# Two VectorE transposes per K tile instead of eight, and TensorE's closing code placed before its loop, in a decode kernel that streams a KV cache

## The chip, the cores and the metric

The kernel runs on one core of a Trainium2 chip. The metric is device microseconds of one execution. A profile is taken of one execution (of before a further one, at 1277.19 us; of each other kernel one of its timed runs). Its span is about 1.3 to 1.6 us shorter than the time of that same execution, and its timestamps are what the traces below show. Before took 1277.59 us (median of 3 runs, 1277.06 to 1277.76) when the prediction was made. All outputs were correct.

## The reference, cut to what matters

One token goes through a mix of two blocks: attention over a cache of 65,536 positions, and a small gated feed-forward block. K and V together are 537 MB of bf16; everything else is 12 MB.

```
x: (1, 1, 448)   k_cache, v_cache: (1, 8, 65536, 256)   wq: (448, 4096)   wo: (4096, 448)
q = x @ wq                                  # 16 heads of 256, two per K/V head
p = softmax(q . k / 16);  o = p . v
a = o.reshape(1, 1, 4096) @ wo
b = ((relu(x @ W_gate)) * (x @ W_up)) @ W_down
g = sigmoid(sum(x * gate_w))
return g * a + (1 - g) * b
```

## The kernel before: the parts that the change touches

K and V come in as 8 MB tiles, 32 of each, into a ring of three buffers. A K tile lands as 128 partitions x 32,768 bf16. VectorE transposes it in place, as uint32, in eight instructions. Scores of the first half of the tile wait for the first four, those of the second half for the last four.

```python
def f_trans(sl, w):
    v = ring[sl][:, w * 4096:(w + 1) * 4096].bitcast(U32)      # 128 x 2048 uint32
    return lambda e: e.transpose(v, v)
# ... (cut) ... for every K tile n in ring slot sl:
kd = dma("sp", t, "r%d" % sl, lambda e, n=n, sl=sl: e.dma_start(ring[sl][:], k_src(n)), free(("k", n)))
tr = [op("dv", tk + 2.22 * w, f_trans(sl, w), [kd]) for w in range(8)]
for b in range(2):
    qk[n, b] = op("pe", tk + (9 * (b + 1) if n else 20 + b), f_qk(n, b, sl), [tr[4 * b + 3], xcopy, ...])
```

The second argument of `op` is a planned time; it only orders the instructions of one engine. VectorE, ScalarE, SyncE and GpSimd run straight code. TensorE has a loop over the heads, between opening code and closing code (last V tiles, output projection):

```python
pl.emit("pe", pe[:heads[0][0]], nc.tensor)       # opening code
pl.emit_loop(H + 1, span, nc.tensor, go)         # the loop; GpSimd gives it one "go" per step
pl.emit("pe", pe[end:], nc.tensor)               # closing code
```

The compiled program has 1940 instructions for TensorE, 465 for VectorE, 186 for GpSimd, 150 for ScalarE, 106 for SyncE.

## Time and profile before

| | before |
|---|---|
| time, span of the profile | 1277.59 us, 1275.7 us |
| moved, mean rate | 549 MB, 430 GB/s over the span |
| DMA share and rate, 200 to 1200 us | 1.00, 433 GB/s |
| VectorE busy, of it transposes | 637 us, 565 us |
| VectorE waiting for K tiles | 390 us |

In all views PE is TensorE's matmuls, PEld its weight loads, DVE VectorE, ACT ScalarE, POOL GpSimd; SPq and PEq are the instruction sequencers of SyncE and TensorE. From the page of before: the slices of DMA (40 equal parts of the span, tenths busy), the queues (packets, MB, share of 16 engines' time) and the costliest group (line, engine, operation, shapes, count, busy us, mean ns, idle before and what ended it).

```profile
DMA  9999999999999999999999999999999999999998
...
q1 hardware_dynamic: 12034, 549.03, 99.6%
q8 instruction: 7, 0.11, 0.0%
q14 instruction: 6, 0.05, 0.0%
...
L369 DVE STREAM_TRANSPOSE ring<-ring 128x2048 uint32<-128x2048 uint32 x256 | 565.4, 2275 | 390.0 <-DMA ring<-in_A_k_cache_dram 390.0
```

The DMA engines are the limit (share 1.00 at 433 GB/s from 200 to 1200 us), and VectorE waits for them (390.0 us). Two queues carry instructions, not data, with a share that rounds to nothing. By what follows, q8 is TensorE's. The 8 KB fetches are q14's.

The stretches of before: bounds in us and length, busy us of PE, PEld, DVE, ACT, POOL, then granted clock, DMA share of 16 engines, GB/s.

```profile
200.00:1200.00 1000.00, 319.73 (x3542) 119.70 (x3534) 503.83 (x313) 48.49 (x94) 0.00 (x0) 0.61 1.00 433
1200.00:1270.00 70.00, 28.77 (x345) 12.25 (x345) 9.07 (x14) 3.14 (x8) 0.00 (x0) 0.68 0.99 421
1270.00:1271.00 1.00, 0.56 (x4) 0.09 (x4) 0.12 (x1) 0.00 (x0) 0.00 (x0) 0.68 0.75 289
1271.00:1272.00 1.00, 0.63 (x8) 0.35 (x8) 0.57 (x1) 0.00 (x0) 0.00 (x0) 0.50 0.33 127
1272.00:1273.00 1.00, 1.00 (x16) 0.53 (x12) 0.16 (x1) 0.00 (x0) 0.00 (x0) 0.50 0.07 25
```

Read the DMA share of the last line: 0.07 is about one engine of sixteen. After 1272 us one DMA engine alone still moves data, and TensorE's last weights wait for it (shown below). With a share of 1.00, in the long stretch, the sixteen move 433 GB/s.

One period of before in the timeline (start us, length us, engine, line, operation, shapes, count, idle time before and its releaser), lines of other engines left out:

```profile
510.67 0.33 SPq L577 DMA_DIRECT2D ring<-in_A_v_cache_dram  x1
...
515.17 0.33 SPq L510 DMA_DIRECT2D ring<-in_A_k_cache_dram  x1
527.88 17.66 DVE L369 STREAM_TRANSPOSE ring<-ring 128x2048 uint32<-128x2048 uint32 x8 [16.51 <-DMA ring<-in_A_k_cache_dram]
```

When the V load is issued at 510.67 us, the K tile queued ahead of it needs until 527.88 us. So in this period 17 us of transfers are queued when a buffer is given back. From that I estimate that a buffer may come up to 17 us later, or sooner, without the queue running dry.

The end of before in the chain of waits (start us, length, what):

```profile
1249.20 22.12 DMA ring<-in_A_wo_dram
1271.33 0.04 issue
1271.37 0.91 PE A_ps L391 x8
1272.28 0.20 PE M_ps L426 x4
1272.48 1.65 PE A_ps L391 x15
1274.12 0.02 issue
1274.15 0.38 DVE P_sb L619
```

The chain merges the last matmuls into one piece (x15) and so hides the last wait. The timeline shows it, at TensorE's last weight loads:

```profile
1273.57 0.09 PEld L391 LDWEIGHTS A_ps<-ring,attnT 128*1 128x1 bf16 x4 [0.30 <-DMA ring<-in_A_wo_dram]
```

They wait for the last piece of `wo`. Its last packet ends at 1273.08 us (next section), and they start 0.5 us later.

### What the DMA records say beyond the views

The trace also holds a record of every DMA packet (start, length, size, queue) but not which of the sixteen engines moved it. It can be worked out. Every engine moves the same 752 packets of the data queue, 80 transfers closed by a 4-byte packet each, and an engine starts a packet within some nanoseconds (mostly 3 to 4 in before) of the end of its last one. Following size and adjacency gives sixteen chains. Their numbering is arbitrary, and two engines that pass within some 10 ns can be exchanged. For each engine I read how far it lies behind the first one when both close the same transfer. Here are the lags of before at the closing of four transfers, each row sorted, and the instruction fetches during data transfer:

```
at   33.8 us: 0 to 0.73
at  138.1 us: 0 .11 .12 .12 .14 .29 .36 .73 .80 1.28 1.67 1.99 2.01 2.02 2.03 2.03
at  447.7 us: 0 .12 .13 .20 .35 .77 .84 .88 1.00 1.66 1.98 2.00 2.01 2.02 2.02 2.28
at 1237.1 us: 0 .12 .26 .35 .41 .92 .98 1.02 1.14 1.71 2.01 2.03 2.05 2.06 2.06 3.39

16 KB (q8, TensorE): 53.9  63.6  70.8  78.1  85.3  106.8  1263.8 us, seven different DMA engines
 8 KB (q14), on the engine that ends last: 58.6  415.1  868.4 us
 8 KB (q14), on three other engines: 426.3  438.2  1254.4 us
last packet of data ends 1273.08 us; the second-to-last engine ends at 1271.77 us
```

A 16 KB fetch leaves its engine about 1.55 us further behind, an 8 KB one 0.97 us (those on the engine that ends last) or 0.7 us (the others). The lag then stays (five engines at 1.99 to 2.03 us at 138.1 us; five at 2.01 to 2.06 at 1237.1), with a DMA share of 1.00 from 200 to 1200 us: no engine idles in which to catch up. The engine with three 8 KB fetches ends 1.3 us after all others.

### The profile page before, as it was taken

How to read it: one execution, taken by the hardware profiler on the slowest of the kernel's cores; microseconds unless marked ns; L12 is line 12 of the kernel's file. 1: busy time of each engine (PE TensorE's matmuls, PEld its weight loads, DVE VectorE, ACT ScalarE, POOL GpSimd, SP SyncE). 2: the span in 40 equal slices, each digit the busy share in tenths (PEclk: the TensorE clock that was granted, in tenths of full speed). 3: DMA queues.
4: the chain of work that ended last, by engine and by line, in shares of the span. 5: the costliest groups of instructions: out<-in, count | busy, mean ns of one | idle time of the engine just before them, and what ended most of it. 6: DMA issues, size and time to landing. Idle time of an engine off the chain costs nothing. (4 is left out here: it accounts for less than half of the span.)

```text
span 1275.7 us, 10235 instructions
## 1 busy us (share of the span) xinstructions
PE 423.0 (33%) x4572; PEld 162.0 (13%) x4572; DVE 636.7 (50%) x432; ACT 63.3 (5%) x124; POOL 4.3 (0%) x21
## 2 busy tenths in 40 slices
PE   3333422334123432225331243322433314233235
PEld 1201110111001210012110111100111101011012
DVE  2697633465533555434555444555435655336600
ACT  0001000010000100001000010000100001000000
POOL 1000000000000000000000000000000000000000
PEclk8656566656566565666665666656666556666667
DMA  9999999999999999999999999999999999999998
GB/s 402 447 427 428 440 429 440 432 429 429 438 440 432 430 429 438 436 432 436 427 429 440 438 432 432 429 438 434 432 438 427 440 429 436 436 429 429 424 437 352
DMA packets 12051, 549.20 MB, mean 430 GB/s; under 512 B 1283, under 2 KB 1798, under 8 KB 3078
## 3 DMA queue, kind: packets, MB, share of 16 engines
q1 hardware_dynamic: 12034, 549.03, 99.6%
q8 instruction: 7, 0.11, 0.0%
q14 instruction: 6, 0.05, 0.0%
q10 hardware_dynamic: 4, 0.00, 0.0%
HBM read 549.03 MB, written 0.00 MB: 430 GB/s over the span
## 5 line engine op out<-in xcount | busy, mean ns | idle before, releaser
L369 DVE STREAM_TRANSPOSE ring<-ring 128x2048 uint32<-128x2048 uint32 x256 | 565.4, 2275 | 390.0 <-DMA ring<-in_A_k_cache_dram 390.0
L380 PE MATMUL ST<-ring,xc 128*16 128x512 bf16 x2048 | 225.2, 613 | 738.4 <-PEq L86 738.4
L380 PEld LDWEIGHTS ST<-ring,xc 128*16 128x16 bf16 x2048 | 68.6, 120 | 880.7 <-issue 879.0
L411 PE MATMUL O<-ring,ptp 128*4 128x512 bf16 x2048 | 150.5, 457 | 36.6 <-PEq L86 24.4
L521 ACT ACTIVATE P_sb<-ST,nmb 128x512 bf16<-128x512 f32 x32 | 45.2, 1412 | 1101.7 <-DVE nmb L519 1101.7
L519 DVE TENSOR_REDUCE nmb<-ST 128x1 f32<-128x512 f32 x32 | 22.0, 689 | 117.8 <-PE ST L380 117.8
L411 PEld LDWEIGHTS O<-ring,ptp 128*4 128x4 bf16 x2048 | 57.5, 100 | 129.1 <-issue 81.3
L421 DVE CAST o_sb<-O 128x512 bf16<-128x512 f32 x8 | 5.5, 691 | 78.2 <-PE O L411 78.2
L540 DVE TENSOR_TENSOR P_sb<-P_sb,hs 128x1024 bf16<-128x1024 bf16 x16 | 18.9, 1221 | 9.6 <-ACT hs L534 9.6
L545 PE MATMUL PT<-identb,P_sb 128*128 128x128 bf16 x128 | 16.2, 307 | 16.8 <-PEq L86 15.8
L545 PEld LDWEIGHTS PT<-identb,P_sb 128*128 128x128 bf16 x128 | 12.4, 138 | 19.2 <-issue 19.2
L554 ACT COPY ptp<-PT 128x256 bf16<-128x256 bf16 x32 | 10.3, 375 | 23.9 <-PE PT L545 23.9
L343 PE MATMUL QN<-ring,P_sb 128*128 128x512 bf16 x32 | 9.9, 486 | 3.9 <-DMA ring<-in_A_wq_dram 3.9
L521 ACT ACTIVATION_READ_ACCUMULATOR P_sb<-ST,nmb 128x1 f32 x32 | 8.4, 262 | 0.0
L458 DVE STREAM_TRANSPOSE scr<-P_sb 128x256 uint32<-128x256 uint32 x1 | 0.4, 445 | 14.3 <-ACT P_sb L457 14.3
L478 PE MATMUL QN<-ring,xT 128*1 128x448 bf16 x16 | 1.7, 568 | 16.1 <-DMA ring<-in_B_W_up_dram 16.1
L433 PE MATMUL M_ps<-emat,o_sb 128*64 128x1 bf16 x112 | 4.5, 199 | 6.6 <-PEq L86 6.6
L530 PE MATMUL M_ps<-identf,hs 128*2 128x128 f32 x8 | 2.6, 321 | 11.1 <-PEq L86 11.1
L440 DVE TENSOR_SCALAR attnT<-M_ps,hs 64x4 bf16<-64x4 f32 x14 | 3.1, 220 | 6.3 <-PE M_ps L433 6.2
L566 DVE RECIPROCAL hs<-M_ps 128x2 f32<-128x2 f32 x8 | 1.4, 170 | 8.3 <-PE M_ps L565 8.3
L433 PEld LDWEIGHTS M_ps<-emat,o_sb 128*64 128x64 bf16 x112 | 4.1, 154 | 9.9 <-issue 9.9
L532 PE MATMUL M_ps<-mx,nselT 2*128 2x1 f32 x16 | 3.6, 292 | 4.1 <-PEq L86 4.1
(80 smaller groups left out, 71.4 us busy)
## 6 DMA issues: line engine op xcount, KB each, us to landing
ring<-in_A_v_cache_dram SPq DMA_DIRECT2D x1, 4096.0 KB, 46.7
ring<-in_A_wq_dram SPq DMA_DIRECT2D x1, 3072.0 KB, 10.6
ring<-in_A_wo_dram SPq DMA_DIRECT2D x1, 2240.0 KB, 37.4
ring<-in_A_v_cache_dram SPq DMA_DIRECT2D x1, 2048.0 KB, 17.8
ring<-in_B_W_down_dram SPq DMA_DIRECT2D x1, 1568.0 KB, 20.8
ring<-in_B_W_gate_dram SPq DMA_DIRECT2D x1, 1344.0 KB, 32.3
ring<-in_B_W_up_dram SPq DMA_DIRECT2D x1, 1344.0 KB, 35.0
ring<-in_A_v_cache_dram SPq DMA_DIRECT2D x1, 1024.0 KB, 19.9
```

Of the source, the lines that this page charges most:

```text
L343: ins = e.matmul(QN_ps, xw3[:, k_, 31 - h:159 - h], rhs, start=(h == 0 and kt == 0), stop=(h == H - 1 and kt == R3))
L369: return lambda e: e.transpose(v, v)
L380: ins = e.matmul(bank[32 * w:32 * w + 16, :], xc[:, x0:x0 + 16], ktv[sl][:, u0:u0 + 16, c, :, r_], start=(b == 0 and c == 0 and r_ == 0), ...
L411: ins = e.matmul(OP[32 * g:32 * g + 4, :], ptp[:, col:col + 13:4], ring[sl][:, base + k * 512:base + (k + 1) * 512], start=(a == 0 and k < ...
L421: o1 = op("dv", tn, lambda e: e.tensor_copy(o_sb[:], OP[:]), [pv[n], last.get(("otr", h - 1))])
L433: ins = e.matmul(T_ps[64 * q:64 * q + 64, s:s + 1], o_sb[:, par * 256 + s:par * 256 + 256:4], emat[:, 2 * par + q:2 * par + q + 1], start= ...
L519: smax[n] = op("dv", tk + 22, lambda e, n=n, NM=NM, t_=t_: e.tensor_reduce(NM[:, t_:t_ + 1], ST[n % 2][:], AX.X, ALU.max, negate=True), [q ...
L521: aexp[n] = op("ac", tk + 23, lambda e, n=n, t_=t_, NM=NM, RS=RS: e.activation(P_sb[:, t_:2048:4], ST[n % 2][:], ACTF.Exp, bias=NM[:, t_:t ...
L532: h5 = mop("pe", T + 15, lambda e, h=h: e.matmul(NMR_ps, nselT[0:2, :], mx2[0:2, 0:1], start=True, stop=True), [h4, l_["ns"]])
L540: rsc = op("dv", tt, lambda e, X=X, pb=pb: e.tensor_tensor(pb, pb, X[:, 12:16].unsqueeze(1).to_broadcast([128, 256, 4]), ALU.mult), [h7, a ...
L545: ins = e.transpose(PT[rd][:, s * 128:(s + 1) * 128], P_sb[:, (rd * 8 + s) * 128:(rd * 8 + s + 1) * 128], identb[:, :])
L554: ins = e.copy(dst, src)
```

## The change

Its intent, as I read it: VectorE gets fewer, longer instructions; and TensorE's closing code is laid in memory before the loop instead of at the very end, so that its fetch leaves the tail. The outer loop runs twice: it skips the closing code and runs the head loop, then comes back and runs the closing code. The arithmetic is the same.

```diff
         def f_trans(sl, w):
-            v = ring[sl][:, w * 4096:(w + 1) * 4096].bitcast(U32)
+            v = ring[sl][:, w * 16384:(w + 1) * 16384].bitcast(U32)
             return lambda e: e.transpose(v, v)
 ...
-                tr = [op("dv", tk + 2.22 * w, f_trans(sl, w), [kd]) for w in range(8)]
+                tr = [op("dv", tk + 8.88 * w, f_trans(sl, w), [kd]) for w in range(2)]
 ...
-                    qk[n, b] = op(... f_qk(n, b, sl), [tr[4 * b + 3], xcopy, ...])
+                    qk[n, b] = op(... f_qk(n, b, sl), [tr[b], xcopy, ...])
 ...
-        pl.emit_loop(H + 1, span, nc.tensor, go)
-        pl.emit("pe", pe[end:], nc.tensor)
+        with nc.tensor.Fori(0, 2) as part:
+            with nc.tensor.If_eq(part.val.handles[0], 1):
+                pl.emit("pe", pe[end:], nc.tensor)
+            with nc.tensor.If_eq(part.val.handles[0], 0):
+                pl.emit_loop(H + 1, span, nc.tensor, go)
```

## The prediction

> **What bounds the kernel.** The DMA queue. The page's slices show DMA at 9 tenths throughout; by stretches it is 1.00 busy at 433 to 434 GB/s from 200 to 1200 us. [...] 549 MB at 434 GB/s is 1265 of the 1275.7 us. The chain of waits ends on the last A_wo pieces, then projections, casts and the store. In each 38.7 us period VectorE waits about 16.5 us for the K tile (waits, timeline). When a period's V load is issued (510.7 us), the K tile ahead of it still has 17 us to run (lands 527.9): the queue never runs dry.
>
> **VectorE.** Eight transposes of 128x2048 uint32 (2275 ns each, one every 2.21 us, 17.66 us per tile) become two of 128x8192. The other size in the trace is 256 elements, 445 ns: slope 1.02 ns an element. Estimate: 8.5 to 8.65 us each, 17.2 per tile; VectorE busy falls from 637 to about 620 us. The first half of the scores still waits for half a tile, 8.6 instead of 8.85 us. None of this is critical: slots come free half a microsecond sooner into a queue with 17 us of work. In tiles 0 to 3 the maximum may wait up to 4 us longer behind a transpose; no load is late for it.
>
> **Instruction fetch, the only way it can show.** The DMA records hold instruction fetches: seven of 16 KB for TensorE (six from 54 to 107 us, one at 1263.8, in the closing code) and 8 KB ones for the others (58.6, 415, 426, 438, 868, 1254 us). Following packets by size and adjacency on each DMA engine, I find that a 16 KB fetch sets its engine back about 1.5 us and an 8 KB one 0.65 to 1; the lag is never made up, since no engine idles. The engine that finishes last got three 8 KB fetches and ends at 1273.08; the next end at 1271.77. Six fewer transposes per tile remove 192 of VectorE's 465 instructions, one to two fetches. If one was on that engine, the end comes up to 1.3 us sooner; then engines that fetched for TensorE are last.
>
> Moving the closing code takes the fetch at 1263.8 out of the tail, but that engine is not the last and TensorE shows no idle time there: about 0. Two jumps are added. [...] The first comes around 61 us, before work ready at 72, the second at 1247, with 10 us of slack before the next V tile (1260.3). A fetch on an already late engine could cost 0.5 to 1.5 us.
>
> **Predicted:** 1276.8 us, 80% range 1274.8 to 1279.0. Faster by over 2%: 0.01; within 2%: 0.98; slower: 0.01.
>
> **What would show it.** Right: 64 transposes of about 8.6 us; VectorE's wait for K half a microsecond longer a tile; DMA still 434 GB/s; no instruction fetch near 1264 us, fewer 8 KB ones; last landing 0 to 1.3 us earlier. Wrong: transposes well over 9 us; DMA share below 1.00 between 200 and 1200; TensorE waiting for its sequencer after 1247; a last engine later than 1273.
>
> **What would make it wrong.** A fetch in the tail that stalls TensorE over 10 us, a transpose much dearer at this size, or fetches piling on one DMA engine.

Two sentences that no run of this case shows are cut from it, where marked; neither is a term of the sum. The sum came to 1276.8 us: 1277.59 us less 0.8, which lies between the 0 and the 1.3 us that the lags allow, with about 0 for the closing code.

## The result, and the profile after

| | before | after |
|---|---|---|
| time, median (range), 6 runs each | 1277.20 us (1277.06 to 1277.76) | 1276.32 us (1276.00 to 1276.48) |
| span of the profile | 1275.7 us | 1275.2 us |
| VectorE busy, of it transposes | 637 us, 565 us | 625 us, 554 us |
| VectorE waiting for K tiles | 390 us | 402 us |
| instructions of VectorE, of TensorE | 465, 1940 | 279, 1952 |

The ratio is 0.9992, 95% interval 0.9979 to 1.0005. A ratio is the mean time of one kernel's runs over that of the other's of the same rounds, so not quite the ratio of the medians. By the interval this is "the same"; the six runs of each do not overlap, and further below the medians of kernels that should be equal, by the theory tested there, agree to 0.2 us (the first result of after, up to 0.34 us higher, is the exception), which is why 0.9 us can be explained at all.

The page of after, the lines that answer to those of before:

```profile
DMA  9999999999999999999999999999999999999998
...
q8 instruction: 7, 0.11, 0.0%
q14 instruction: 5, 0.04, 0.0%
...
L369 DVE STREAM_TRANSPOSE ring<-ring 128x8192 uint32<-128x8192 uint32 x64 | 553.9, 8691 | 402.5 <-DMA ring<-in_A_k_cache_dram 402.5
```

VectorE gave back 11.5 us of transposes and waits 12.5 us longer for K tiles: the saved time became waiting. One 8 KB fetch less is the other difference on this page. The stretches of after:

```profile
200.00:1200.00 1000.00, 318.63 (x3546) 118.86 (x3538) 495.46 (x159) 48.48 (x94) 0.00 (x0) 0.61 1.00 433
...
1270.00:1271.00 1.00, 0.27 (x8) 0.13 (x6) 0.69 (x1) 0.00 (x0) 0.00 (x0) 0.77 0.71 272
1271.00:1272.00 1.00, 1.00 (x14) 0.50 (x12) 0.04 (x1) 0.00 (x0) 0.00 (x0) 0.50 0.33 124
1272.00:1273.00 1.00, 1.00 (x12) 0.48 (x8) 0.13 (x1) 0.00 (x0) 0.00 (x0) 0.50 0.04 14
```

The long stretch is the same to the GB/s. Again one engine is alone after 1272 us, and it stops sooner (share 0.04 instead of 0.07). By the DMA records it is not VectorE's engine any more. The timeline and the end of the chain of after:

```profile
528.31 17.30 DVE L369 STREAM_TRANSPOSE ring<-ring 128x8192 uint32<-128x8192 uint32 x2 [16.87 <-DMA ring<-in_A_k_cache_dram]
```

```profile
1247.32 23.46 DMA ring<-in_A_wo_dram
1270.78 0.04 issue
1270.82 0.91 PE A_ps L391 x8
1271.73 0.20 PE M_ps L426 x4
1271.93 1.67 PE A_ps L391 x15
1273.59 0.02 issue
1273.62 0.38 DVE P_sb L619
```

TensorE's last weight loads, in the timeline of after:

```profile
1273.04 0.09 PEld L391 LDWEIGHTS A_ps<-ring,attnT 128*1 128x1 bf16 x4 [0.29 <-DMA ring<-in_A_wo_dram]
```

The whole tail stands 0.5 us earlier and is otherwise the same chain. By the DMA records, VectorE's engine has two fetches (131.0 and 869.8 us) in place of three and lies 2.15 us behind at 1237 us (3.39 in before), no 16 KB fetch stands near 1264 us, and the last packet ends at 1272.58 us. The engine that ends last, 2.78 us behind, is another one: it was late from the start and then fetched for TensorE (see "The full change again"). This profile is of the slowest of the six runs of after (1276.48 us).

### The profile page after: what moved, and what is told of

Read it like the earlier page. It is cut to its first block, busy times and chain, and to the rows that moved or that the text cites. A ratio compares the mean times of both kernels' runs of the same rounds, so it can differ in the third digit from the quotient of the medians.

```text
span 1275.2 us, 10054 instructions
## 1 busy us (share of the span) xinstructions
PE 420.1 (33%) x4572; PEld 160.9 (13%) x4572; DVE 625.3 (49%) x240; ACT 63.3 (5%) x124; POOL 4.6 (0%) x21
## 5 line engine op out<-in xcount | busy, mean ns | idle before, releaser
L369 DVE STREAM_TRANSPOSE ring<-ring 128x8192 uint32<-128x8192 uint32 x64 | 553.9, 8691 | 402.5 <-DMA ring<-in_A_k_cache_dram 402.5
L391 PE MATMUL A_ps<-ring,attnT 128*1 128x224 bf16 x64 | 4.7, 305 | 1.3 <-DMA ring<-in_A_wo_dram 0.7
```

The costliest lines, as they stand in the source:

```text
L391: ins = e.matmul(A_ps[32 * g:32 * g + 1, 0:D2], lhsT, rhs[:, g * D2:(g + 1) * D2], start=start, stop=stop, skip_group_check=True, tile_pos ...
```

## The experiments

Theory A: the DMA is the limit, and the execution ends when the DMA engine that is furthest behind ends. VectorE's instruction fetches all go to one DMA engine; fewer instructions mean fewer fetches there. Rival B: the gain comes from the moved closing code. Rival C: it comes from the shorter time that VectorE needs per tile. Rival D: it is noise. All runs are timed in 5 rounds. The first four ran on one chip with 9 runs of before (median 1277.20 us), the last four likewise (1277.13 us).

### Transposes only

The diff of the change without its last part; the closing code stays behind the loop.

> Only the two-instruction transposes; the closing code stays behind the loop. Theory A (fewer VectorE instruction fetches on the DMA engine that ends last): the whole gain, 0.5 to 1.2 us under before (ratio 0.9990 to 0.9996); two fetches of the VectorE kind in place of three, the 16 KB fetch near 1264 us still there. Rival B (the moved closing code gives the gain): ratio 1.0000, within 0.2 us. Rival C (shorter VectorE time per tile gives it): the same gain as A, so this run does not tell A from C.

Measured: 1275.98 us (1275.82 to 1276.03), ratio 0.9990. The 16 KB fetch is still in the tail, at 1263.0 us; VectorE's engine has two fetches (128.7, 867.5 us) and ends 2.1 us behind the first one, level with the engines that fetched for TensorE. The last packet ends at 1272.02 us, 1.06 us before that of before. The whole gain is here. B falls.

### Closing code only

```diff
-        pl.emit_loop(H + 1, span, nc.tensor, go)
-        pl.emit("pe", pe[end:], nc.tensor)
+        with nc.tensor.Fori(0, 2) as part:
+            ...   (as in the change; transposes as before)
```

> Only the moved closing code, eight transposes. Theory A: no gain, within 0.3 us of before (ratio 0.9998 to 1.0003), three VectorE fetches on one DMA engine, which ends last by about 1.3 us; no 16 KB fetch near 1264 us. Rival B: the whole gain, ratio about 0.9993. Both: TensorE enters its loop several us late (first scores in the loop at about 79 us, not 73.5), at no cost in time.

Measured: 1277.09 us (1276.98 to 1277.24), ratio 1.0000. The 16 KB fetch has left the tail and nothing came of it. VectorE's engine has its three fetches again (56.0, 417.4, 868.3 us), stands 3.08 us behind at 1237 us, where the next stands 2.12, and is alone at the end, as a stretch of this run shows:

```profile
1272.00:1273.00 1.00, 1.00 (x16) 0.67 (x16) 0.16 (x1) 0.00 (x0) 0.00 (x0) 0.50 0.06 22
```

The new layout, with its jump over the closing code, does cost TensorE time. Here is its first score group inside the loop, in the timeline of before, then of this run:

```profile
73.54 3.59 PE L380 MATMUL ST<-ring,xc 128*16 128x512 bf16 x32 [12.78 <-PEq L86]
```

```profile
81.03 5.35 PE L380 MATMUL ST<-ring,xc 128*16 128x512 bf16 x53 [20.61 <-PEq L86]
```

7.5 us later (I had written about 79 us), with fetches of 16 KB at 63.4, 70.7, 78.0 and 85.5 us beside it. The queued transfers cover it (ratio 1.0000). The delay is about one interval between these fetches (7.3 to 7.5 us); that TensorE waits for exactly one such fetch more is not shown.

### 32 transposes per tile: the dose raised

```diff
-            v = ring[sl][:, w * 4096:(w + 1) * 4096].bitcast(U32)
+            v = ring[sl][:, w * 1024:(w + 1) * 1024].bitcast(U32)
 ...
-                tr = [op("dv", tk + 2.22 * w, f_trans(sl, w), [kd]) for w in range(8)]
+                tr = [op("dv", tk + 0.555 * w, f_trans(sl, w), [kd]) for w in range(32)]
 ...  (the scores wait for tr[16 * b + 15])
```

> Dose up: 32 transposes of 128x512 per K tile, 1233 VectorE instructions instead of 465, closing code as before. Theory A: about six more 8 KB fetches than the three of before, all on the same DMA engine, each setting it back 0.97 us: the last landing and the time 5 to 6 us later (1282 to 1283.5 us, ratio 1.0039 to 1.005), while the other DMA engines end where they did and DMA stays near 1.00 busy. Rival C (VectorE time): VectorE takes about 19.4 us a tile instead of 17.66, and the time follows those 1.8 us per tile (tens of us) or not at all, with no single DMA engine standing out. Rival D (noise): no difference beyond 0.3 us.

Measured: 1282.88 us (1282.73 to 1283.04), ratio 1.0045, interval 1.0031 to 1.0058. Stretches of this run:

```profile
200.00:1200.00 1000.00, 315.14 (x3526) 117.78 (x3518) 533.98 (x920) 48.65 (x94) 0.00 (x0) 0.61 1.00 434
...
1272.00:1273.00 1.00, 0.10 (x4) 0.00 (x0) 0.00 (x0) 0.00 (x0) 0.00 (x0) 1.00 0.07 29
1273.00:1275.00 2.00, 0.86 (x12) 0.20 (x12) 0.00 (x0) 0.00 (x0) 0.00 (x0) 1.00 0.06 25
1275.00:1278.00 3.00, 1.64 (x18) 0.51 (x15) 0.69 (x1) 0.00 (x0) 0.00 (x0) 0.62 0.07 26
1278.00:1279.00 1.00, 0.97 (x16) 0.64 (x16) 0.16 (x1) 0.00 (x0) 0.00 (x0) 0.50 0.05 20
```

Up to 1272 us nothing is changed: share 1.00 and 434 GB/s in the long stretch, though VectorE works 30 us more in it. Then one engine of sixteen runs alone for almost seven microseconds. Its fetches, nine 8 KB ones about 127 to 146 us apart once the tiles run, add up step by step:

```
lag of VectorE's DMA engine:  1.29 at 61 us (1 fetch)   2.26 at 138 (2)   3.21 at 293 (3)   4.18 at 448 (4)
                              6.14 at 680 (6)   7.14 at 873 (7)   8.14 at 970 (8)   9.17 at 1237 (9)
the next engine at 1237 us: 2.18
```

Six more fetches than before (768 more instructions, so 128 each) made it 5.7 us longer: 0.95 us each. (Two of the nine, at 537 and 934 us, came out on another engine's number in the packet-following; the lag steps put them on this one.) If C held, VectorE's 1.4 us more per tile (19.10 us against 17.66) would have shown in the long stretch. Rival D falls as well.

### The instructions back, the short transposes kept

```diff
+        fill = sb("fill", [1, 192], F32)
 ...
+                tr = [op("dv", tk + 8.88 * w, f_trans(sl, w), [kd]) for w in range(2)]
+                for w in range(6):
+                    op("dv", tk + 8.88 + 0.01 * w + 0.01, lambda e, k=6 * n + w: e.memset(fill[:, k:k + 1], 0.0))
```

Each memset has its own element.

> Two transposes per tile plus six one-element memsets per tile right after them: VectorE time as short as after (about 17.3 us a tile before the memsets), but 465 instructions as in before; closing code as before. The result is still correct. Theory A: no gain, three VectorE fetches, within 0.3 us of before (ratio 0.9998 to 1.0003). Rival C: the gain stays, ratio about 0.9993.

Measured: 1277.10 us (1277.04 to 1277.27), ratio 1.0000. Two groups of this run:

```profile
L370 DVE STREAM_TRANSPOSE ring<-ring 128x8192 uint32<-128x8192 uint32 x64 | 553.9, 8691 | 403.3 <-DMA ring<-in_A_k_cache_dram 403.3
...
L515 DVE MEMSET fill<- 1x1 f32 x192 | 4.6, 59 | 0.0
```

The transposes are exactly those of after, VectorE waits for K as in after, and the gain is gone. What came back is the number of instructions, 465, and the third fetch on VectorE's engine (58.5, 417.5, 868.4 us; largest lag 3.22 us at 1237 us, the next 2.15). C falls: 192 memsets of 59 ns, 4.6 us of VectorE time in all and far from any critical wait, take back the whole 1.1 us (1275.98 us with transposes only, 1277.10 us here).

### Fetches of another engine: four, then 28 copies per tile on ScalarE

If what counts is the latest DMA engine, a fetch on an early one is free. Base is the transposes-only kernel.

```diff
+        fill = sb("fill", [1, 128], BF)          # 896 in the second
 ...
+                for w in range(4):               # 28 in the second
+                    op("ac", tk + 31 + 0.01 * w, lambda e, k=4 * n + w: e.copy(fill[:, k:k + 1], ones_f[0:1, 0:1]), [c_one])
```

> Base is the transposes-only kernel (1275.98 us, two VectorE fetches, last DMA engine 2.12 us behind the first). ScalarE gets four one-element copies more per K tile: 278 instructions in place of 150, one block of 128 more. Theory A, in its form 'the latest engine counts, not the sum': one fetch more on ScalarE's DMA engine, which stands at about 0.7 us and goes to 1.3 to 1.7, still below 2.1: time as the base, within 0.2 us (ratio to before 0.9988 to 0.9993). Rival ('every fetch costs its time'): 0.65 to 1 us slower than the base, about 1276.8.

Measured: 1276.16 us (1275.85 to 1276.24), ratio 0.9992. ScalarE's DMA engine had two fetches (206.1, 826.0 us) and stood at 1.55 us; VectorE's stood at 2.30 and ended last. The extra fetch cost nothing clear of noise (0.1 us over the kernels of these rounds that lack it).

> The same with 28 copies more per K tile: 1046 ScalarE instructions, seven blocks more. Theory A: seven more fetches on ScalarE's DMA engine, 0.65 to 1 us each; that engine passes all others, ends 3 to 5.5 us later than the base's last one: 1279 to 1281.5 us, ratio to before 1.0014 to 1.0035. VectorE's engine stays where it was. If the cost is special to VectorE or to the transposes: time as the base, 1276.

Measured: 1279.35 us (1279.25 to 1279.60), ratio 1.0018, interval 1.0004 to 1.0032. Eight fetches on ScalarE's DMA engine set it back to 5.58 us, 0.69 each, past all others (VectorE's: 2.25); the last packet ends at 1275.36 us. Stretches of this run:

```profile
1270.00:1272.00 2.00, 0.99 (x12) 0.20 (x12) 0.00 (x0) 0.00 (x0) 0.00 (x0) 1.00 0.58 224
1272.00:1273.00 1.00, 0.39 (x4) 0.09 (x4) 0.00 (x0) 0.00 (x0) 0.00 (x0) 1.00 0.07 29
1273.00:1275.00 2.00, 1.02 (x16) 0.65 (x18) 0.85 (x2) 0.00 (x0) 0.00 (x0) 0.94 0.06 24
```

Again one engine alone at the end. So this is not special to VectorE or to transposes: ScalarE's instruction stream does it too, and its fetches are free until their DMA engine becomes the last. GpSimd and SyncE were not tried.

### One transpose per tile

```diff
-            v = ring[sl][:, w * 16384:(w + 1) * 16384].bitcast(U32)
+            v = ring[sl][:, w * 32768:(w + 1) * 32768].bitcast(U32)
 ...  (range(1); both halves of the scores wait for tr[0])
```

> Base is the transposes-only kernel with one transpose of 128x16384 per K tile: both halves of the scores wait for the whole tile. 241 VectorE instructions in place of 273. Theory A: still two VectorE fetches or one; last engine then one that fetched for TensorE at about 2.0 us, so the time is that of the base within 0.3 us (1275.7 to 1276.3). The scores start 8.6 us later and the K buffer is free about 3.6 us later, inside the 17 us of queued transfers: no cost. If slack were thinner than read from the trace, the DMA share falls below 1.00 and the time rises by more than 1 us.

Measured: 1276.09 us (1275.96 to 1276.44), ratio 0.9993. Two fetches for VectorE (131.1, 1024.7 us), lag 2.14 us. The long stretch of this run:

```profile
200.00:1200.00 1000.00, 272.97 (x3542) 119.97 (x3530) 494.48 (x133) 48.59 (x94) 0.00 (x0) 0.62 1.00 433
```

Waiting for the whole tile costs nothing, as the estimate of 17 us of queued transfers said. It gains nothing either.

### The full change again

> The changed kernel again on the chip of these runs. Theory A: 1276.0 to 1276.5, as it was. If the difference between the transposes-only kernel and the full change (1275.98 against 1276.32) is real, this one is 0.2 to 0.4 us slower than the transposes-only kernel; if it is chance, within 0.15 us of it.

Measured: 1276.03 us (1275.86 to 1276.26), ratio 0.9991. It is level with transposes only (1275.98 us in the other rounds): the 0.34 us between their first results did not come back, so it is not a difference of the kernels that these runs show. The profile of the first result, one execution and its slowest, shows a possible source: one DMA engine was already 1.2 us behind at 30 us, before any fetch during the stream that could explain it, and then got a 16 KB fetch; it ended last at 1272.58 us. In this second profile no engine stood over 0.5 us behind at 34 us, and the last packet ends at 1272.08 us. Why the engines start unevenly is open.

All runs together (packet end and lag from the profiled run, time from all runs; in after the largest lag is not that of VectorE's engine, which is 2.15):

| kernel | fetches on VectorE's DMA engine | largest lag at 1237 us | last packet ends | time |
|---|---|---|---|---|
| before | 3 | 3.39 | 1273.08 | 1277.20 / 1277.13 |
| closing code only | 3 | 3.08 | 1272.88 | 1277.09 |
| memsets added | 3 | 3.22 | 1273.00 | 1277.10 |
| after | 2 | 2.78 | 1272.58 | 1276.32 |
| after again | 2 | 2.26 | 1272.08 | 1276.03 |
| transposes only | 2 | 2.12 | 1272.02 | 1275.98 |
| one transpose | 2 | 2.14 | 1272.06 | 1276.09 |
| 4 copies on ScalarE | 2 | 2.30 | 1272.21 | 1276.16 |
| 28 copies on ScalarE | 2 (ScalarE's: 8) | 5.58 | 1275.36 | 1279.35 |
| 32 transposes | 9 | 9.17 | 1278.84 | 1282.88 |

The profiled execution's own time minus its last packet is 3.9 to 4.2 us in every row. No version ran that is clear of the full change: with two fetches VectorE's engine is nearly level with those that fetched for TensorE, and a further gain would have to come from there or from the uneven start. That was not tried.

## Why the prediction was right

- **The bound.** Right: 433 to 434 GB/s and share 1.00 between 200 and 1200 us in before, after and the runs whose long stretch is shown. VectorE could be loaded by 46 us more (32 transposes) or start the scores half a tile later (one transpose) without a mark in that stretch.
- **The transposes.** 8.69 us each, where I had 8.5 to 8.65; 17.30 us per tile, where I had 17.2. VectorE busy is 625 us, not 620: my 17.2 us per tile took a saving of 0.08 us per instruction removed. Measured, eight to two saves 0.36 us, 0.06 per instruction. The tile times of the traces, 19.10, 17.66, 17.30 and 17.25 us for 32, 8, 2 and 1 instructions, fit 17.18 us plus 0.06 us per instruction within 0.01 us, an estimate from these four runs. It fits the pace of the stream, not the duration of one short instruction (2275 ns on average with eight per tile, against 17.66 / 8 = 2.21 us). The wait for K grew by 0.39 us a tile; I had said about half a microsecond.
- **The gain and its cause.** The step "one to two fetches less; if one was on the engine that ends last, the end comes up to 1.3 us sooner; then engines that fetched for TensorE are last" held but for its last clause. In the profile of after an engine that fetched for TensorE was last, helped by its late start; but in after again, one transpose and 4 copies on ScalarE it was still VectorE's, by about 0.15 to 0.3 us (lags of 2.26, 2.14 and 2.30 us at 1237 us), and with transposes only the two are level. One fetch was gone, 0.97 us of lag, and the time fell by 0.9 us in the first rounds and 1.1 in the second, against the 0.8 implied by 1276.8 from 1277.59. It was argued from lags in one trace; the 32 transposes, the memsets and the ScalarE copies showed it. That one of the fetches removed would be on that engine was left at an "if", and 0.8 us lies between the two outcomes (0 and 1.3 us). The 80% range, 4.2 us wide, holds the time of before as well, so the mechanism was tested by the runs and not by the range.
- **The closing code: about 0.** Right (0.1 us, inside the spread). The step about the first jump was wrong in its size: I let it be over by 72 us, and TensorE entered the loop at 79.4 us in after (81.0 in closing code only), against 73.5 in before. Nothing depended on it. What TensorE waits for in that later entry (5.8 to 7.5 us) is not shown: no run isolates it. At the jump back after 1245 us TensorE's weight loads waited 1.1 us in after, where before shows no gap and with no 16 KB fetch near it; I had listed waiting there as a sign against me, but it is followed by a wait of 10.4 us for the next V tile (9.8 us in before), which is longer.

## What to carry to other kernels

In these runs the DMA was saturated (share 1.00 between 200 and 1200 us wherever that stretch is shown), and instruction fetches competed with the data. Each went through one of the sixteen DMA engines and set it back 0.7 to 1.55 us, and that engine's lag lasted to the end. So count instructions, also on engines with much idle time: ScalarE is busy for 5% of the span of before, and with 28 copies per tile instead of 4 the time rose from 1276.16 to 1279.35 us. The last microseconds of DMA share told whether one engine ended alone (0.06 to 0.07); if it does, find whose instructions it fetched, and change their number, not their duration (192 memsets of 59 ns took back 1.1 us). Time saved on an engine that waits for a saturated queue came back as waiting (11.5 us saved, 12.5 us more wait): check how many microseconds of transfers are queued before you value it.

## What the traces show of instruction fetches

- In the run with 32 transposes per tile, with nine fetches for VectorE, all 353.9 us of idle time before its transposes end with the landing of a K tile; no wait for instructions shows there. What the fetch does is displace data on one DMA engine: by 1.55 us for TensorE's 16 KB, 0.97 us for VectorE's 8 KB, 0.69 us for ScalarE's 8 KB, where a packet of 8 KB of data takes 0.31 us in before. Why the cost is two to three times that of the bytes, and differs between VectorE and ScalarE, no run here shows.
- The fetches other than TensorE's are packets of 8 KB, for VectorE one per 128 instructions (768 more gave six more), all of VectorE's on one DMA engine, while TensorE's seven 16 KB fetches in before fell on seven.
- With the jump over the closing code and otherwise the kernel of before, TensorE entered its loop 7.5 us later beside a saturated queue (81.03 against 73.54 us).
